# Every pair of a 512-token chunk takes seven products, and four of its accumulators are copied out before the joins

## The chip, the cores and the metric

The kernel runs on one core of one Trainium2 chip. A core has TensorE (PE: matrix products, with a weight load of its own, PEld), VectorE (DVE), ScalarE (ACT), GpSimd (POOL) and queues that issue transfers (SP's among them). Each takes its instructions in the order in which the program wrote them, and they meet at semaphores. The metric is the device time of one execution in microseconds, as the median of several runs.

## The reference

Two stages stand one behind the other. The first is a Fourier mix: `X = rfft(x)` along 3008 tokens, `Yr = Xr @ w_r - Xi @ w_i + b_r` and `Yi = Xr @ w_i + Xi @ w_r + b_i`, a soft threshold at 0.01 on both, and `irfft`. The second works on all 4 x 3008 = 12032 tokens of 256 channels: `h = x @ w_in` (256 to 2048), `g = max(h, 0) + alpha * min(h, 0)`, `out = g @ w_out` (2048 to 256). All of it is float32. The change touches the second stage alone.

## The kernel before

Every product is made of three matmuls in a faster float format: a number is split into a high and a low part, and high x high, high x low and low x high are summed in PSUM. Splitting is work for the other engines: ScalarE copies a tile into the high format, VectorE or GpSimd subtracts that copy from the tile and so gets the low part.

The first 700 us or so hold the Fourier mix of all four batches and the second stage for 12 chunks of 256 or 384 tokens. Then come 14 chunks of 512 tokens (`n` from 0 to 13) and one of 384 tokens. The change is in these.

A chunk of 512 tokens is done in 8 *pairs* of 128-wide feature blocks (`t` from 0 to 7). One turn `k` of the last loop of the program writes, in this order:

- `s_l1` of pair `k`, the first layer: 2 x 6 matmuls of 512 columns on TensorE into two PSUM banks `ps_h` (a pool of two, L785). ScalarE takes `Relu(-ps)` from each bank (L788) and VectorE makes `g` from that and the bank (L789, "the activation"). That VectorE instruction is the last reader of its bank, and the first layer of the next pair needs the bank again.
- `s_l2` of pair `k - 2`, the second layer. The two feature blocks, the two halves of the tokens and the two halves of the output channels make a 2 x 2 by 2 x 2 block product, done by Winograd's scheme in 7 products instead of 8. Each product is 3 matmuls of 256 columns (L886 to L888): 21 matmuls. They add into seven halves of four banks over the 8 pairs of a chunk: `a[0]`, `a[1]`, `b[0]`, `b[1]` (tag `o`), `c[0]`, `c[1]` (tag `f`), and `o_last[0]`.
- `s_out`, behind the last pair of a chunk: ScalarE copies three accumulators to SBUF (L911 to L913), VectorE joins all of them to the four blocks of the output (L914 to L921, eight instructions).
- `s_sums` of pair `k`: from the activation `g` the operands of the 7 products are made. ScalarE writes the high part `dh` of three of the four blocks (L804), VectorE the sums `t13` (L816) and `t24` (L818, L820) and the low part `dl` (L819); ScalarE the high parts `h13` (L821) and `h24` (L822) of the sums, VectorE `l13` (L823) and GpSimd `l24` (L824). The high and the low tiles have two buffers each, so pair `k` writes where pair `k - 2` is read by the products of the same turn.
- `s_turn`, two turns after `s_out`: four transposes of the joined blocks (L930), whose result is then stored.

In some turns the 16 matmuls of a down-transform (L611) that brings new tokens stand ahead of `s_l1`.

One pair of each chunk is *plain*: `t = 1` (`PLAIN = (1,)`). It takes 8 ordinary block products, 24 matmuls, no `t13`, `t24`, `h24`, `l24`, and half of `h13` and `l13` (L807 to L809). Its sums are made in the very turn that has the `s_out` of the chunk before. Because two of its products go to the fourth quarter block alone, it uses an eighth accumulator, `o_last[1]`.

Of the kernel before, what the change touches and what calls it, by code (L numbers as in the profile page):

```python
# [93 lines left out]
def fft_mix_moe(ctx, tc, x, w_r, w_i, b_r, b_i, w_in, w_out, alpha, la, rb, lc, rd, lf, cf, sel, out):  # L94
# [38 lines left out]
    def f(t):  # L133
        return t.bitcast(F32)
# [599 lines left out]
    HS = SC // 2  # L734
# [55 lines left out]
                                   op0=ALU.mult, op1=ALU.add)  # L790
        sq[n, t] = q

    def s_sums(n, t):
        q = sq.pop((n, t))
        if n == NS2 - 1:
            z_parts(t, q)
# [6 lines left out]
        l13 = work.tile([128, 2, HS], F32R, tag="Yh", name="l13")  # L803
        A.activation(out=dh, in_=q[:, HS:], func=AF.Copy)  # L804
        d = [(dh[:, HS * k:HS * k + HS], dl[:, HS * k:HS * k + HS]) for k in range(3)]
        if t in PLAIN:
            A.activation(out=h13[:, 0], in_=b12, func=AF.Copy)  # L807
            V.tensor_tensor(out=dl, in0=q[:, HS:], in1=f(dh), op=ALU.subtract)
            V.tensor_tensor(out=l13[:, 0], in0=b12, in1=f(h13)[:, 0], op=ALU.subtract)  # L809
            sg[n, t] = d + [(h13[:, 0], l13[:, 0])]  # L810
            return
        t13 = work.tile([128, 2, HS], F32, tag="zst", name="t13")
        t24 = work.tile([128, 2, HS], F32, tag="bt", name="t24", bufs=3)
        h24 = work.tile([128, 2, HS], F32R, tag="xl", name="h24")
# [4 lines left out]
        V.tensor_tensor(out=dl, in0=q[:, HS:], in1=f(dh), op=ALU.subtract)  # L819
        V.tensor_tensor(out=t24[:, 1], in0=b21, in1=t24[:, 0], op=ALU.subtract)  # L820
        A.activation(out=h13, in_=t13, func=AF.Copy)  # L821
        A.activation(out=h24, in_=t24, func=AF.Copy)  # L822
        V.tensor_tensor(out=l13, in0=t13, in1=f(h13), op=ALU.subtract)  # L823
        G.tensor_tensor(out=l24, in0=t24, in1=f(h24), op=ALU.subtract)  # L824
# [47 lines left out]
    def s_l2(n, t):  # L872
        if t == 0:
            sa[n] = [ps_o.tile([128, 2, HS], F32, tag="o", name="ps_o") for _ in range(2)] \
                + [ps_f.tile([128, 2, HS], F32, tag="f", name="ps_o")]
        a, b, c = sa[n]
        r, z = t == 0, t == PR - 1

        def block(j, h):
            m = 2 * t + j  # L880
            w = wo_h[m // FH][:, m % FH].rearrange("p w (c h) -> p w h c", h=2)
            return w[:, 0, h], w[:, 1, h]

        def run(prods):
            for (wh, wl), (gh, gl), o, first, last in prods:
                PE.matmul(o, wh, gh, start=first, stop=False)  # L886
                PE.matmul(o, wl, gh, start=False, stop=False)  # L887
                PE.matmul(o, wh, gl, start=False, stop=last)  # L888

        if t in PLAIN:  # L890
            b11, b22, b21, b12 = sg.pop((n, t))
            run([(block(j, h), g, o, False, False) for h, bs, o in (
                (0, (b11, b21), a[:, 1]), (0, (b12, b22), b[:, 0]),
                (1, (b11, b21), o_last[:, 0]), (1, (b12, b22), o_last[:, 1])) for j, g in enumerate(bs)])
            return
        b11, b22, b21, t1, t3, t2, t4 = sg.pop((n, t))
        s1, s2, s3, s4 = ([x[:, t] for x in sw[k]] for k in range(4))
        run([(block(0, 0), b11, a[:, 0], r, False), (block(1, 0), b21, a[:, 1], False, z),
             (s4, b22, b[:, 0], r, False), (s3, t3, b[:, 1], False, z),
             (s1, t1, c[:, 1], r, False), (s2, t2, c[:, 0], False, z),  # L900
             (block(1, 1), t4, o_last[:, 0], r, z)])

    so = {}

    def s_out(n):
        a, b, c = sa.pop(n)
        e = [work.tile([128, HS], F32, tag="q", name="se", bufs=3) for _ in range(3)]
        u = [work.tile([128, HS], F32, tag="gh", name="su", bufs=4) for _ in range(4)]
        c1 = work.tile([128, 2, HS], F32, tag="Yt", name="c1", bufs=1)
        c2 = work.tile([128, 2, HS], F32, tag="Yc", name="c2", bufs=1)  # L910
        A.activation(out=e[0], in_=a[:, 0], func=AF.Copy)  # L911
        A.activation(out=e[1], in_=c[:, 1], func=AF.Copy)
        A.activation(out=e[2], in_=o_last[:, 1], func=AF.Copy)  # L913
        V.tensor_tensor(out=c1[:, 1], in0=a[:, 1], in1=e[0], op=ALU.add)  # L914
        V.tensor_tensor(out=u[0], in0=c[:, 0], in1=e[0], op=ALU.add)
        V.tensor_tensor(out=u[1], in0=e[2], in1=e[1], op=ALU.subtract)
        V.tensor_tensor(out=u[2], in0=u[0], in1=e[1], op=ALU.subtract)
        V.tensor_tensor(out=u[3], in0=b[:, 1], in1=u[0], op=ALU.add)
        V.tensor_tensor(out=c1[:, 0], in0=b[:, 0], in1=u[2], op=ALU.add)
        V.tensor_tensor(out=c2[:, 1], in0=o_last[:, 0], in1=u[3], op=ALU.add)  # L920
        V.tensor_tensor(out=c2[:, 0], in0=u[3], in1=u[1], op=ALU.add)  # L921
        so[n] = c1, c2

    def s_turn(n):
# [31 lines left out]
    BO = {1: 49, 2: 86, 3: 123}  # L956
    BP = 3
    SLAG = 2
    PLAIN = (1,)
    MP = [3, 4, 4, 4, 4, 5, 5, 6]  # L960
    CM = 8
    BL = 4
# [19 lines left out]
    with tc.manual_schedule():  # L982
# [199 lines left out]
        for i in range(NS):  # L1182
# [7 lines left out]
            if i < NS - 1:  # L1190
                do(todo, i)
        for k in range(len(spairs) + SLAG):
            do(pre, k)
            if k < len(spairs):
                s_l1(*spairs[k])
# [6 lines left out]
            if k >= SLAG:  # L1202
                n, t = spairs[k - SLAG]
                if n == NS2 - 1:
                    z_l2(t)
                else:
                    s_l2(n, t)
                    if t == PR - 1:
                        s_out(n)
            if k < len(spairs):  # L1210
                s_sums(*spairs[k])
            if k >= SLAG and t == 1 and n:
                s_turn(n - 1)
        assert not pre and not post
# [32 lines left out]
```

## Time and profile before

| | us |
|---|---|
| median of 3 runs | 1357.33 (1357.21 to 1358.26) |
| the profiled execution, whole | 1358.56 |
| its span, first to last instruction | 1356.8 |
| PE busy, share of the span | 1341.8 (99%) |
| DVE busy | 1036.9 (76%) |
| ACT busy | 760.7 (56%) |
| POOL busy | 382.7 (28%) |

A matmul's row is longer than the time until the next one starts, since they overlap: a matmul of 256 columns has a row of 0.28 us, and the next starts about 0.12 us later. So the cost of a product on TensorE is read from the starts, not from the rows. A row of VectorE or ScalarE that stands for several instructions has "x2", "x4" behind it; "idle before" in brackets is the time that the engine stood still, and what ended it.

### The profile page before, as it was taken

The numbers are of one execution on the slowest core, as the hardware profiler recorded it, in microseconds if no ns is written. First come the engines' busy times: TensorE is split into PE (matmuls) and PEld (weight loads), VectorE is DVE, ScalarE is ACT, GpSimd is POOL, SyncE is SP. The second block draws the span as 40 slices with busy tenths as digits, with TensorE's granted clock in tenths as the row PEclk, the third lists the DMA queues.
The fourth block names the chain that finished last, engine by engine and source line by source line (L and its number), as shares of the span: only waits on it lengthen the run. The fifth ranks groups of instructions, "written<-read, shape, count | busy, mean of one in ns | idle before, by whom it ended". The sixth has DMA issues, their size and how long they took to land.

```text
span 1356.8 us, 25103 instructions
## 1 busy us (share of the span) xinstructions
PE 1341.8 (99%) x9208; PEld 1253.9 (92%) x9208; DVE 1036.9 (76%) x1930; ACT 760.7 (56%) x1528; POOL 382.7 (28%) x404
## 2 busy tenths in 40 slices
PE   9999999999999999999999999999999999999998
PEld 5979899999999999999999999999999999999998
DVE  2766856777777777776768888888888888888885
ACT  3566555565566645545556555555565555555553
POOL 4855832222222222222212211212112111211222
PEclk9999999999999999999999999999999999999999
DMA  9965223342334322111110110110011101110001
GB/s 239 255 176 154 80 83 109 91 135 90 100 97 130 94 68 82 47 59 47 36 36 1 39 28 1 40 28 19 13 37 29 28 6 35 28 28 8 21 17 28
DMA packets 88118, 89.66 MB, mean 66 GB/s; under 512 B 42317, under 2 KB 70448, under 8 KB 87995
## 3 DMA queue, kind: packets, MB, share of 16 engines
q1 hardware_dynamic: 79428, 76.76, 20.0%
q0 software_dynamic: 5168, 8.02, 2.3%
q10 hardware_dynamic: 3399, 3.27, 0.8%
q8 instruction: 73, 1.20, 0.4%
q14 instruction: 50, 0.41, 0.1%
HBM read 50.49 MB, written 34.34 MB: 63 GB/s over the span
## 4 chain that ended last, share of the span: by engine, by line
PE 92%; DVE 2%; DMA 2%; ACT 1%; issue 1%; POOL 0%; ACTq 0%; SPq 0%; DVEq 0%; POOLq 0%
PE ps_h L785 24%; PE ps_h L680 13%; PE ps_m L486 6%; PE ps_o L887 6%; PE ps_o L888 6%; PE ps_o L886 6%; PE ps_d L611 4%; PE ps_o L719 3%; PE ps_o L718 3%; PE ps_o L717 3%; PE ps_b L426 3%; PE ps_a L387 2%; PE o_last L719 1%; PE o_last L717 1%; PE o_last L718 1%; PE o_last L886 1%
## 5 line engine op out<-in xcount | busy, mean ns | idle before, releaser
L785 PE MATMUL ps_h<-yh,w 128*128 128x512 f32 (+1 forms) x960 | 315.6, 389 | 0.0
L824 POOL TENSOR_TENSOR l<-t,h 128x512 fp32r<-128x512 f32 x98 | 127.1, 1297 | 496.5 <-ACT h L822 452.7
L785 PEld LDWEIGHTS ps_h<-yh,w 128*128 128x128 f32 x960 | 180.0, 188 | 33.2
L789 DVE SCALAR_TENSOR_TENSOR sq<-sq,beta_s,ps_h 128x512 f32<-128x512 f32 (+1 forms) x240 | 168.0, 733 | 55.1 <-ACT sq L788 54.4
L680 PE MATMUL ps_h<-yh,w 128*128 128x384 f32 (+1 forms) x704 | 206.0, 335 | 1.3 <-DVE q L687 1.2
L785 PE MATMUL ps_h<-yl,w 128*128 128x512 f32 (+1 forms) x480 | 186.3, 388 | 0.0
L691 ACT ACTIVATE gh<-q 128x384 fp32r<-128x384 f32 (+1 forms) x192 | 99.2, 516 | 145.9 <-DVE q L687 144.6
L687 DVE SCALAR_TENSOR_TENSOR q<-q,beta_s,ps_h 128x384 f32<-128x384 f32 (+1 forms) x192 | 115.5, 601 | 81.8 <-ACT q L686 80.2
L692 POOL TENSOR_TENSOR gl<-q,gh 128x384 fp32r<-128x384 f32 (+1 forms) x91 | 98.3, 1081 | 266.6 <-ACT gh L691 253.4
L804 ACT ACTIVATE dh<-sq 128x768 fp32r<-128x768 f32 x112 | 94.8, 846 | 118.0 <-DVE sq L789 74.9
L788 ACT ACTIVATE sq<-ps_h 128x512 f32<-128x512 f32 (+1 forms) x240 | 133.2, 586 | 27.4 <-PE ps_h L785 25.9
L680 PEld LDWEIGHTS ps_h<-yh,w 128*128 128x128 f32 x704 | 129.3, 189 | 3.9 <-issue 1.3
L822 ACT ACTIVATE h<-t 128x512 fp32r<-128x512 f32 x98 | 62.0, 633 | 104.4 <-DVE t L820 101.1
L680 PE MATMUL ps_h<-yl,w 128*128 128x384 f32 (+1 forms) x352 | 116.4, 331 | 0.0
L686 ACT ACTIVATE q<-ps_h 128x384 f32<-128x384 f32 (+1 forms) x192 | 91.6, 477 | 39.5 <-PE ps_h L680 36.8
L719 PE MATMUL ps_o<-w,gl 128*128 128x256 f32 x384 | 108.5, 283 | 3.3 <-POOL gl L692 3.3
L718 PE MATMUL ps_o<-w,gh 128*128 128x256 f32 x384 | 108.4, 282 | 0.0
L717 PE MATMUL ps_o<-w,gh 128*128 128x256 f32 x384 | 108.1, 282 | 0.0
L785 PEld LDWEIGHTS ps_h<-yl,w 128*128 128x128 f32 x480 | 90.5, 189 | 13.6
L819 DVE TENSOR_TENSOR dl<-sq,dh 128x768 fp32r<-128x768 f32 x98 | 93.4, 953 | 3.7 <-ACT dh L804 3.6
L888 PE MATMUL ps_o<-l,sw_a 128*128 128x256 f32 x294 | 82.0, 279 | 0.0
L886 PE MATMUL ps_o<-h,sw_a 128*128 128x256 f32 x294 | 81.9, 279 | 0.0
(211 smaller groups left out, 3628.7 us busy)
## 6 DMA issues: line engine op xcount, KB each, us to landing
zt<-zd SPq DMA_DIRECT2D x32, 384.0 KB
ad<-ast SPq DMA_DIRECT2D x48, 192.0 KB
bt<-ad SPq DMA_DIRECT2D x72, 128.0 KB
zd<-zst SPq DMA_DIRECT2D x36, 256.0 KB
xt<-in_x SPq DMA_DIRECT2D x21, 320.0 KB
out<-oT SPq DMA_DIRECT2D x152, 32.0 KB
cw_s<-in_moe_w_in SPq DMA_DIRECT2D x8, 512.0 KB
cw_s<-in_moe_w_out SPq DMA_DIRECT2D x8, 512.0 KB
```

The lines of the kernel that those rows point to most:

```text
L680: PE.matmul(ps, wi_h[m // FH][:, w, ct, 128 * (m % FH):128 * (m % FH) + 128], a[:, ct, 0:n], start=(k == 0), stop=(k == 3 * CT - 1))
L687: V.scalar_tensor_tensor(out=q, in0=q, scalar=beta_s[:, m:m + 1], in1=ps, op0=ALU.mult, op1=ALU.add)
L691: A.activation(out=hi, in_=q, func=AF.Copy)
L717: PE.matmul(a, hi[:, t], w[:, 0], start=(i, k) in first, stop=False)
L718: PE.matmul(a, hi[:, t], w[:, 1], start=False, stop=False)
L719: PE.matmul(a, lo[:, t], w[:, 0], start=False, stop=(i, k) in last)
L785: PE.matmul(ps, wi_h[m // FH][:, w, ct, 128 * (m % FH):128 * (m % FH) + 128], a[:, ct, 0:w1], start=(k == 0), stop=(k == 3 * CT - 1))
L788: A.activation(out=q[:, j], in_=ps, func=AF.Relu, scale=-1.0)
L789: V.scalar_tensor_tensor(out=q[:, j], in0=q[:, j], scalar=beta_s[:, m:m + 1], in1=ps, op0=ALU.mult, op1=ALU.add)
L824: G.tensor_tensor(out=l24, in0=t24, in1=f(h24), op=ALU.subtract)
L886: PE.matmul(o, wh, gh, start=first, stop=False)
L888: PE.matmul(o, wh, gl, start=False, stop=last)
```

## The change

- `PLAIN` goes: all 8 pairs of a chunk take 7 products. `o_last[1]` is no longer used by them.
- The 7 products are written in another order: first the one to `o_last[0]`, then `c[1]`, `c[0]`, `a[0]`, `a[1]`, `b[0]`, `b[1]`. Before it was `a[0]`, `a[1]`, `b[0]`, `b[1]`, `c[1]`, `c[0]`, `o_last[0]`.
- `s_out` is cut in two. ScalarE now makes four copies (`a[0]`, `c[1]`, `o_last[0]`, `b[0]`), written inside `s_sums` between `h13` and `h24`; VectorE's joins are seven instead of eight, and stand behind all of `s_sums`. The copies go to four buffers of another tag.
- In the turns of the 384-token chunk, whose `s_sums` is another function, the copies stand ahead of it.

```diff
-        if t in PLAIN:
-            A.activation(out=h13[:, 0], in_=b12, func=AF.Copy)
-            V.tensor_tensor(out=dl, in0=q[:, HS:], in1=f(dh), op=ALU.subtract)
-            V.tensor_tensor(out=l13[:, 0], in0=b12, in1=f(h13)[:, 0], op=ALU.subtract)
-            sg[n, t] = d + [(h13[:, 0], l13[:, 0])]
-            return
...
         A.activation(out=h13, in_=t13, func=AF.Copy)
+        if ends is not None:
+            s_copy(ends)
         A.activation(out=h24, in_=t24, func=AF.Copy)
...
-        if t in PLAIN:
-            b11, b22, b21, b12 = sg.pop((n, t))
-            run([(block(j, h), g, o, False, False) for h, bs, o in (
-                (0, (b11, b21), a[:, 1]), (0, (b12, b22), b[:, 0]),
-                (1, (b11, b21), o_last[:, 0]), (1, (b12, b22), o_last[:, 1])) for j, g in enumerate(bs)])
-            return
...
-        run([(block(0, 0), b11, a[:, 0], r, False), (block(1, 0), b21, a[:, 1], False, z),
-             (s4, b22, b[:, 0], r, False), (s3, t3, b[:, 1], False, z),
+        run([(block(1, 1), t4, o_last[:, 0], r, z),
              (s1, t1, c[:, 1], r, False), (s2, t2, c[:, 0], False, z),
-             (block(1, 1), t4, o_last[:, 0], r, z)])
+             (block(0, 0), b11, a[:, 0], r, False), (block(1, 0), b21, a[:, 1], False, z),
+             (s4, b22, b[:, 0], r, False), (s3, t3, b[:, 1], False, z)])
...
+    def s_copy(n):
+
+        a, b, c = sa[n]
+        se[n] = []
+        for p in (a[:, 0], c[:, 1], o_last[:, 0], b[:, 0]):
+            t = work.tile([128, HS], F32, tag="gl", name="se", bufs=4)
+            A.activation(out=t, in_=p, func=AF.Copy)
+            se[n].append(t)
 
     def s_out(n):
...
-        A.activation(out=e[0], in_=a[:, 0], func=AF.Copy)
-        A.activation(out=e[1], in_=c[:, 1], func=AF.Copy)
-        A.activation(out=e[2], in_=o_last[:, 1], func=AF.Copy)
-        V.tensor_tensor(out=c1[:, 1], in0=a[:, 1], in1=e[0], op=ALU.add)
-        V.tensor_tensor(out=u[0], in0=c[:, 0], in1=e[0], op=ALU.add)
-        V.tensor_tensor(out=u[1], in0=e[2], in1=e[1], op=ALU.subtract)
-        V.tensor_tensor(out=u[2], in0=u[0], in1=e[1], op=ALU.subtract)
-        V.tensor_tensor(out=u[3], in0=b[:, 1], in1=u[0], op=ALU.add)
-        V.tensor_tensor(out=c1[:, 0], in0=b[:, 0], in1=u[2], op=ALU.add)
-        V.tensor_tensor(out=c2[:, 1], in0=o_last[:, 0], in1=u[3], op=ALU.add)
-        V.tensor_tensor(out=c2[:, 0], in0=u[3], in1=u[1], op=ALU.add)
+        for o, x, y, op in ((u2, c[:, 0], p1, ALU.add), (c1[:, 1], a[:, 1], p1, ALU.add),
+                            (u3, b[:, 1], u2, ALU.add), (u4, u2, p5, ALU.subtract),
+                            (c2[:, 1], u3, p4, ALU.add), (c1[:, 0], u4, p3, ALU.add),
+                            (c2[:, 0], u3, p5, ALU.subtract)):
+            V.tensor_tensor(out=o, in0=x, in1=y, op=op)
...
-    PLAIN = (1,)
...
                     s_l2(n, t)
-                    if t == PR - 1:
-                        s_out(n)
+                    ends = n if t == PR - 1 else None
             if k < len(spairs):
-                s_sums(*spairs[k])
+                last = spairs[k][0] == NS2 - 1
+                if last and ends is not None:
+                    s_copy(ends)
+                s_sums(*spairs[k], None if last else ends)
+            if ends is not None:
+                s_out(ends)
```

What the change does to the order on the engines is shown at one place, the turn in which the last products of chunk 1 and the sums of pair 1 of chunk 2 stand together; it is the same in the other chunks. On VectorE, before: the activations of the pair (L789), the eight joins (L914 to L921), the two low parts of the plain pair, and the next pair's activations.

```order
L789 SCALAR_TENSOR_TENSOR sq<-sq,beta_s,ps_h 128x512 x2
L914 TENSOR_TENSOR c_9807<-ps_o,se 128x256
L915 TENSOR_TENSOR su<-ps_o,se 128x256
L916 TENSOR_TENSOR su<-se 128x256
L917 TENSOR_TENSOR su<-su,se 128x256
L918 TENSOR_TENSOR su<-ps_o,su 128x256
L919 TENSOR_TENSOR c_9807<-ps_o,su 128x256
L920 TENSOR_TENSOR c_9808<-o_last,su 128x256
L921 TENSOR_TENSOR c_9808<-su 128x256
L808 TENSOR_TENSOR dl<-sq,dh 128x768
L809 TENSOR_TENSOR l_9823<-sq,h_9822 128x256
L789 SCALAR_TENSOR_TENSOR sq<-sq,beta_s,ps_h 128x512 x2
```

The same place on VectorE after the change, from the sum `t24` of the pair on (its `t13`, L810, and the activations stand ahead of these rows): L812 to L819 are the five instructions that every pair has now, L916 are the joins.

```order
L812 TENSOR_TENSOR t_9818<-sq,t_9817 128x256
L813 TENSOR_TENSOR dl<-sq,dh 128x768
L814 TENSOR_TENSOR t_9818<-sq,t_9818 128x256
L819 TENSOR_TENSOR l_9815<-t_9817,h_9814 128x512
L916 TENSOR_TENSOR su<-ps_o,se 128x256
L916 TENSOR_TENSOR c_9840<-ps_o,se 128x256
L916 TENSOR_TENSOR su<-ps_o,su 128x256
L916 TENSOR_TENSOR su<-su,se 128x256
L916 TENSOR_TENSOR c_9841<-su,se 128x256
L916 TENSOR_TENSOR c_9840<-su,se 128x256
L916 TENSOR_TENSOR c_9841<-su,se 128x256
L789 SCALAR_TENSOR_TENSOR sq<-sq,beta_s,ps_h 128x512 x2
```

Between the activations of one pair and those of the next there stood 8 + 2 instructions; now there are 5 + 7, and the joins have moved from the front of this stretch to its end.

On ScalarE, before: the two Relu of the pair (L788), three copies (L911 to L913), the high parts of the plain pair, and the next pair's Relu.

```order
L788 ACTIVATE sq<-ps_h 128x512 x2
L911 ACTIVATE se<-ps_o 128x256
L912 ACTIVATE se<-ps_o 128x256
L913 ACTIVATE se<-o_last 128x256
L804 ACTIVATE dh<-sq 128x768
L807 ACTIVATE h_9822<-sq 128x256
L788 ACTIVATE sq<-ps_h 128x512 x2
```

The same place after the change: `dh` (L804), `h13` (L815), four copies (L903), `h24` (L818).

```order
L788 ACTIVATE sq<-ps_h 128x512 x2
L804 ACTIVATE dh<-sq 128x768
L815 ACTIVATE h_9814<-t_9817 128x512
L903 ACTIVATE se<-ps_o 128x256 x2
L903 ACTIVATE se<-o_last 128x256
L903 ACTIVATE se<-ps_o 128x256
L818 ACTIVATE h_9819<-t_9818 128x512
L788 ACTIVATE sq<-ps_h 128x512 x2
```

The copies stand behind `dh` and `h13` now and ahead of `h24`. On TensorE the end of a pair's products, before:

```order
L888 MATMUL ps_o<-l_9746,sw_a 128x256
L886 MATMUL ps_o<-h_9750,sw_a 128x256
L887 MATMUL ps_o<-h_9750,sw_a 128x256
L888 MATMUL ps_o<-l_9751,sw_a 128x256
L886 MATMUL o_last<-h_9750,w_253 128x256
L887 MATMUL o_last<-h_9750,w_253 128x256
L888 MATMUL o_last<-l_9751,w_253 128x256
L785 MATMUL ps_h<-yh,w_253 128x512
```

and after, with `h_9757` as `h13` and `dh` as the high part of the three blocks of that pair:

```order
L884 MATMUL ps_o<-dl,w_253 128x256
L882 MATMUL ps_o<-dh,sw_a 128x256
L883 MATMUL ps_o<-dh,sw_b 128x256
L884 MATMUL ps_o<-dl,sw_a 128x256
L882 MATMUL ps_o<-h_9757,sw_a 128x256
L883 MATMUL ps_o<-h_9757,sw_b 128x256
L884 MATMUL ps_o<-l_9758,sw_a 128x256
L785 MATMUL ps_h<-yh,w_253 128x512
```

The tiles `dh` and `dl` were read by products 1 to 3 of 7; now they are read by products 4 to 6.

## Rows read from the trace of the kernel before

**Rows 1.** Busy time by stretch: length, busy of each engine (instructions), clock, DMA.

```profile
157.05:160.46 3.41, 3.23 (x12) 3.23 (x13) 1.84 (x3) 1.01 (x2) 2.99 (x4) 0.50 0.00 0
...
108.00:113.00 5.00, 3.83 (x31) 3.65 (x30) 2.71 (x8) 2.77 (x10) 1.90 (x4) 1.00 0.93 320
699.00:1320.00 621.00, 621.00 (x4017) 566.87 (x4016) 533.63 (x1005) 360.71 (x697) 127.36 (x99) 1.00 0.10 24
```

**Rows 2.** Timeline of TensorE, chunk 2: start us, length us, engine, line, operation.

```profile
782.39 0.40 PE L785 MATMUL ps_h<-yh,w 128*128 128x512 f32 x1
...
785.14 0.28 PE L886 MATMUL ps_o<-dh,w 128*128 128x256 f32 x1
...
787.62 0.40 PE L785 MATMUL ps_h<-yh,w 128*128 128x512 f32 x1
...
795.60 0.28 PE L886 MATMUL ps_o<-dh,w 128*128 128x256 f32 x1
...
798.23 0.28 PE L887 MATMUL o_last<-dh,w 128*128 128x256 f32 x1
...
798.47 0.39 PE L785 MATMUL ps_h<-yh,w 128*128 128x512 f32 x1
...
803.69 1.92 PE L611 MATMUL ps_d<-rd_s,zt 96*128 96x94 f32 x16
805.40 0.48 PE L785 MATMUL ps_h<-yh,w 128*128 128x512 f32 x1
```

**Rows 3.** Groups by line from 600 us on: xcount | busy, mean ns | idle before.

```profile
L808 DVE TENSOR_TENSOR dl<-sq,dh 128x768 fp32r<-128x768 f32 x14 | 13.3, 952 | 1.3 <-ACT dh L804 1.3
```

**Rows 4.** Timeline of VectorE over one ordinary pair.

```profile
826.47 1.40 DVE L789 SCALAR_TENSOR_TENSOR sq<-sq,beta_s,ps_h 128x512 f32<-128x512 f32 x2 [0.67 <-ACT sq L788]
...
830.25 0.68 DVE L823 TENSOR_TENSOR l<-t,h 128x512 fp32r<-128x512 f32 x1
831.60 0.75 DVE L789 SCALAR_TENSOR_TENSOR sq<-sq,beta_s,ps_h 128x512 f32<-128x512 f32 x1 [0.67 <-ACT sq L788]
```

**Rows 5.** Timeline of VectorE in chunk 2: joins, plain pair, transposes.

```profile
785.23 1.50 DVE L789 SCALAR_TENSOR_TENSOR sq<-sq,beta_s,ps_h 128x512 f32<-128x512 f32 x2 [0.67 <-ACT sq L788]
...
787.87 0.42 DVE L915 TENSOR_TENSOR su<-ps_o,se 128x256 f32<-128x256 f32 x1 [0.81 <-ACT se L912]
...
790.24 0.95 DVE L808 TENSOR_TENSOR dl<-sq,dh 128x768 fp32r<-128x768 f32 x1
...
800.64 0.68 DVE L823 TENSOR_TENSOR l<-t,h 128x512 fp32r<-128x512 f32 x1
801.24 1.42 DVE L930 STREAM_TRANSPOSE oT<-c 128x256 f32<-128x256 f32 x4
802.59 1.36 DVE L789 SCALAR_TENSOR_TENSOR sq<-sq,beta_s,ps_h 128x512 f32<-128x512 f32 x2
```

**Rows 6.** Timeline of ScalarE: a copy, a high part, a pair's Relu.

```profile
787.82 0.38 ACT L913 ACTIVATE se<-o_last 128x256 f32<-128x256 f32 x1
...
798.55 0.85 ACT L804 ACTIVATE dh<-sq 128x768 fp32r<-128x768 f32 x1 [1.54 <-PE o_last L887]
...
830.99 1.07 ACT L788 ACTIVATE sq<-ps_h 128x512 f32<-128x512 f32 x2
```

**Rows 7.** Timeline of all engines at pair 1 of chunk 5.

```profile
918.08 0.40 PE L785 MATMUL ps_h<-yh,w 128*128 128x512 f32 x1
...
921.67 0.75 DVE L789 SCALAR_TENSOR_TENSOR sq<-sq,beta_s,ps_h 128x512 f32<-128x512 f32 x1 [0.66 <-ACT sq L788]
```

**Rows 8.** Timeline of all engines where TensorE waits for a bank.

```profile
110.69 0.48 DVE L687 SCALAR_TENSOR_TENSOR q<-q,beta_s,ps_h 128x256 f32<-128x256 f32 x1
...
111.31 0.41 PE L680 MATMUL ps_h<-yh,w 128*128 128x384 f32 x1 [1.18 <-DVE q L687]
...
111.56 0.34 PE L680 MATMUL ps_h<-yl,w 128*128 128x384 f32 x1
```

**Rows 9.** Timeline of TensorE at its longest wait behind the start.

```profile
157.23 0.58 PE L719 MATMUL ps_o<-w,gl 128*128 128x256 f32 x1 [2.62 <-POOL gl L692]
```

More of the change, by code (lines that the diff above doesn't have):

```diff
@@ L791, in s_l1, with s_sums @@
         sq[n, t] = q
-    def s_sums(n, t):
+    def s_sums(n, t, ends=None):
         q = sq.pop((n, t))
@@ L900, in s_l2 @@
              (s1, t1, c[:, 1], r, False), (s2, t2, c[:, 0], False, z),
-             (block(1, 1), t4, o_last[:, 0], r, z)])
+             (block(0, 0), b11, a[:, 0], r, False), (block(1, 0), b21, a[:, 1], False, z),
+             (s4, b22, b[:, 0], r, False), (s3, t3, b[:, 1], False, z)])
     so = {}
+    se = {}
+    def s_copy(n):
[5 more added lines that the diff above has]
+            se[n].append(t)
@@ L905, in s_out @@
     def s_out(n):
         a, b, c = sa.pop(n)
-        e = [work.tile([128, HS], F32, tag="q", name="se", bufs=3) for _ in range(3)]
-        u = [work.tile([128, HS], F32, tag="gh", name="su", bufs=4) for _ in range(4)]
+        p1, p5, p4, p3 = se.pop(n)
+        u2, u3, u4 = (work.tile([128, HS], F32, tag="gh", name="su", bufs=4) for _ in range(3))
         c1 = work.tile([128, 2, HS], F32, tag="Yt", name="c1", bufs=1)
         c2 = work.tile([128, 2, HS], F32, tag="Yc", name="c2", bufs=1)
-        A.activation(out=e[0], in_=a[:, 0], func=AF.Copy)
@@ L1192, in fft_mix_moe @@
         for k in range(len(spairs) + SLAG):
+            ends = None
             do(pre, k)
```

## The prediction, made before the changed kernel was run

> **What bounds the kernel now.** I read the busy times by stretch first. From 699 to 1320 us, where all 512-token chunks lie, TensorE is busy for 621.00 of 621.00 us at the full one of its two clocks, 2.4 GHz (granted 1.00), VectorE for 534, ScalarE for 361 [rows 1]. So nothing that another engine saves can shorten this stretch; only less work on TensorE can, and only as long as nobody makes it wait. The next view is TensorE's timeline, read by starts. A pair takes 782.39 to 787.62 = 5.23 us, of which its 21 second-layer matmuls take 785.14 to 787.62 = 2.48. The plain pair's 24 take 795.60 to 798.47 = 2.87 [rows 2]. The third is VectorE over one ordinary pair: from one activation to the next it is 831.60 - 826.47 = 5.13 us [rows 4]. That is only 0.10 less than TensorE's 5.23. VectorE is therefore a second bound that lies just under the first, and the question is what it has to carry at a chunk's end.
>
> **What goes.** 14 plain pairs [rows 3] at 2.87 - 2.48 = 0.39 us: 5.5 us less on TensorE. This much is certain if TensorE never stands still.
>
> **What comes back.** The plain pair is not only dearer on TensorE, it is cheaper on VectorE, and its sums fall in the very turn that holds the joins. There VectorE loses one join and two low parts and gets the five instructions of a full pair. I work out when the first activation behind the joins is done, because the second next first layer needs the bank that it reads. On VectorE, behind the start of a pair's first activation: its l13 starts 830.25 - 826.47 = 3.78 later [rows 4], and the next instruction can start 801.24 - 800.64 = 0.60 behind that [rows 5]; the seven joins take what seven instructions take before, 787.87 to 790.24 = 2.37 [rows 5]; the activation takes 0.75 [rows 4]. The hand-over to TensorE I take from the one place where it waited for such a bank: the activation ended at 110.69 + 0.48 = 111.17, TensorE started at 111.31, so 0.14 [rows 8]. The nearest other hand-over, TensorE to ScalarE, bounds it from below: 798.23 + 0.28 = 798.51 to 798.55, 0.04 [rows 2, 6]. I take 0.14, since it is the same pair of engines and the same kind of wait.
>
> Path 1, VectorE being late. If the pair's first activation starts L behind its first layer, the bank is free at L + 3.78 + 0.60 + 2.37 + 0.75 + 0.14 = L + 7.64; TensorE wants it at 2 x 5.23 = 10.46. It stands still for L - 2.82. In chunk 2, L is 785.23 - 782.39 = 2.84 [rows 2, 5]; in chunk 5 it is 921.67 - 918.08 = 3.59 [rows 7]; in the 13 chunks that follow another one it lies between 2.83 and 3.59, and is over 3.27 in five of them.
>
> Path 2, a wait that the change adds. `dh` is written over a buffer that the products of the same turn read. Before, product 3 of 7 was its last reader, now it is product 6, whose second matmul is the 17th of the 21. ScalarE takes `dh` 0.04 after such a matmul [rows 2, 6]. Behind `dh`, ScalarE has h13, the copies, h24 and the next pair's Relu queued, VectorE has dl, l13, the joins and that activation. From the start of the products: 16 x 2.48 / 21 = 1.89, + 0.28 + 0.04 = 2.21 until `dh` starts; l13 starts 800.64 - 798.55 = 2.09 behind it in a pair where `dh` was late [rows 5, 6]; then 0.60 + 2.37 + 0.75 + 0.14: 8.16. TensorE wants the bank at 2.48 + 5.23 = 7.71. It stands still for 0.45 even where VectorE has no lag. In the other turns there are no joins (2.37 less), and this wait costs nothing.
>
> So the stall at each of the 13 joins is the larger of 0.45 and L - 2.82: eight times 0.45, five times 0.48 to 0.77, 6.9 in all (0.53 each). A matmul that has waited starts slowly: the one at 111.31 has a row of 0.41 against 0.34 for the next [rows 8]; 13 x 0.07 = 0.9. That is 7.8 us at this place. The 14th plain pair opens the first chunk, where there is nothing to join; I take 0 there.
>
> A second place follows. When TensorE restarts, VectorE is exactly late: the next activations start 0.89 before, 4.24 behind (5.13 on) and, past the pair with the four transposes (802.59 - 801.24 = 1.35 [rows 5]), at 4.24 + 3.78 + 0.60 + 1.35 = 9.97. With 0.89 the bank is free at 10.86; TensorE wants it at 10.46 + 0.07. Another 0.33, with the slow start 0.40. In six of the 13 chunks the 16 down-transform matmuls stand just there and give 805.40 - 803.69 = 1.71 [rows 2]; seven remain: 2.8 us.
>
> **What I cost at nothing.** The fourth copy and its place: four copies of 0.38 are 1.5 us, and if all of it came ahead of the next Relu (830.99 [rows 6]), the activation could start at 831.60 + 1.5 = 833.1; VectorE, busy with joins, arrives at 830.85 + 2.37 = 833.2. Covered, by 0.1 at worst. The accumulators: behind the products' start, `o_last` is free once the third copy ends, by 2.21 + 0.85 + 0.63 + 3 x 0.38 = 4.8 (the middle term, for h13, is my estimate from the Relu of that width, 1.07 for two [rows 6]); the next chunk writes it at 2.48 + 2.75 = 5.23. `a` is free with the second join, 2.21 + 2.09 + 0.60 + 0.34 + 0.42 + 0.14 = 5.8, and wanted nine matmuls on, at 6.3. `b` comes later still. Where path 1 is later than path 2, by 0.3 at most, this still holds, with 0.2 left. GpSimd's l24 is now read by the first product instead of the last two, a pair and a half after it is made; its 14 more instructions fall in its idle time (127 us busy of 621 [rows 1]).
>
> **Sum.** 7.8 + 2.8 - 5.5 = +5.1 us: 1363.7 against the profiled execution's 1358.56. The median of the runs shown lies 1.23 below that execution, so I forecast 1357.33 + 5.1 = 1362.4. Ends: with a hand-over of 0.04 and no slow start the stalls are 13 x 0.43 + 7 x 0.23 = 7.2, the sum +1.7, 1359.0. If each join took its whole row of 0.42 (7 x 0.42 = 2.94 instead of 2.37), 7.4 more come at the first place: 1369.8. I stay near the middle because the joins are written so that neighbours don't wait for each other.
>
> **Rivals.**
> *Shorter waits.* The same two places, with the price at its lower end: 1359.0, within 0.2%. For it: the balance is fine, a mean stall of 0.39 per chunk already eats the gain. Against: the only wait of this kind cost 0.14 and a slow start [rows 8].
> *No stall.* VectorE is early enough, and only the 5.5 us remain: 1351.8. The mechanism would be that the copies are now ahead of the joins, so that VectorE no longer waits for ScalarE among them (0.81 at 787.87 [rows 5]), and gains on TensorE by 0.10 in each pair. It decides at the turn of the joins: they would have to end 0.45 earlier than in path 2 and L to stay under 2.82. For it: L is close to that in several chunks. Against: path 2 doesn't hang on how early VectorE is, and the 0.81 was a wait in a turn with little else to do.
> *The clock.* The wait of 2.62 at 157.23 [rows 9] was followed by 3.41 us at the lower clock, 1.2 GHz (granted 0.50), while that of 1.18 at 111.31 [rows 8] lies in a stretch at 1.00 [rows 1]. If each of the 20 stalls cost such a stretch, half of 3.41 would be lost 20 times: +34, 1396. Against: the stalls are 0.4 to 0.8 long. The Trainium skill (TensorE: Matmul & The Clock Gate, "A second HAM failure mode: psum-queue depth-cycling") says that short idle times between groups of matmuls, as a kernel goes round its PSUM banks, can make the clock swing between both levels. By that rule this rival is the one to come; the trace shows it for the long wait alone, and no row shows it for a short one.
>
> **How the numbers follow.** The forecast 0.61, shorter waits 0.21, no stall 0.14, the clock 0.04. What a measurement of this kernel can tell from no change is 0.2%, 2.7 us. Slower is the forecast and the clock, 0.65; the same is the shorter waits, 0.21; faster is no stall, 0.14. The forecast's own range is 1359 to 1368. To leave out no more than 2 in 10 it has to reach down past the shorter waits to part of the way to no stall, 1354; above, I stop at 1368, short of the upper end of the joins.
>
> **What would show it.** TensorE's idle time by line should be new at L785 alone, with VectorE's L789 as its cause, some 0.4 to 0.8 us at pair 3 of every chunk and again at pair 5 where no down-transform stands ahead; between these, pairs of 5.23. VectorE's first activation behind the joins should start about 4.8 to 5.1 us behind its first layer. `dh` should wait for TensorE's L883 in the turn of the joins. No matmul at L882 to L884 should wait. I am wrong if those activations start under 4.3 us behind, if the first product of a chunk waits for a copy or a join, or if the clock falls.

## The result, and the profile after

The changed kernel takes 1369.26 us (median of 4 runs, 1367.84 to 1369.72) against 1357.80 for the kernel before (4 runs beside it): ratio 1.0083, 95% interval 1.0065 to 1.0100. It is slower, as forecast, but by 11.5 us where 5.1 were forecast, and it lies above the range. The profiled span is 1367.6 us, 10.8 longer. The mean granted clock is 0.998, and 1.00 in the stretch of the 512-token chunks, so the 1.2 GHz level has no part in it. The row shows the length of the stretch, busy time of TensorE, its loads, VectorE, ScalarE and GpSimd, the clock and DMA:

```profile
710.00:1330.00 620.00, 609.74 (x3913) 553.83 (x3912) 548.88 (x1020) 359.86 (x711) 142.39 (x111) 1.00 0.09 22
```

Before, TensorE was busy for all of such a stretch [rows 1]; now it stands still for 10.3 of 620 us.

The page gives the busy time by engine. VectorE is busy for 23.6 us more than before and GpSimd for 17.4; TensorE has 42 matmuls less.

```profile
PE 1340.3 (98%) x9166; PEld 1249.6 (91%) x9166; DVE 1060.5 (78%) x1958; ACT 766.9 (56%) x1556; POOL 400.1 (29%) x418
```

Then the chain that ended last, by engine. Before, TensorE held 92% of it and VectorE 2%; now VectorE is on it for 9%.

```profile
PE 84%; DVE 9%; issue 3%; ACT 2%; DMA 1%; DVEq 0%; POOL 0%; ACTq 0%; SPq 0%
```

The third view is the groups by line, for TensorE's first layer: busy time and mean ns, then the idle time before it. Before, no idle time stood here.

```profile
L785 PE MATMUL ps_h<-yh,w 128*128 128x512 f32 (+1 forms) x960 | 317.2, 391 | 11.4 <-DVE sq L789 10.9
```

That row undercounts, since a matmul's length in the trace covers part of a short gap. I therefore read the starts in TensorE's timeline, group by group, and split the difference of the two spans. Place 1 is the first layer of a chunk's pair 3 and place 2 that of pair 5, the two places of the prediction:

| Part | us |
|---|---|
| second-layer products, 112 groups: 277.9 against 242.7 + 40.2 (98 ordinary, 14 plain) | -4.95 |
| place 1: 13 waits of 0.87 to 1.09 | +11.8 |
| place 2: 7 waits of 0.20 to 0.24 | +1.6 |
| the turn of the last chunk: one wait | +1.3 |
| slow first matmuls behind these 21 waits, 0.10 each | +2.2 |
| first layers apart from that, 120 groups, 0.011 shorter each | -1.4 |
| before the first of these layers | +0.3 |
| sum | +10.8 |

So every wait of the 512-token chunks is one that the prediction named, but the first place costs 13.1 us with its slow starts, not 7.8. Chunk 2 shows why. These are the start of a pair's products (L882) and the first layers of three pairs in TensorE's timeline (start, length, engine, line):

```profile
785.47 0.28 PE L882 MATMUL o_last<-h,w 128*128 128x256 f32 x1
...
787.95 0.40 PE L785 MATMUL ps_h<-yh,w 128*128 128x512 f32 x1
...
794.03 0.50 PE L785 MATMUL ps_h<-yh,w 128*128 128x512 f32 x1 [0.71 <-DVE sq L789]
...
799.38 0.40 PE L785 MATMUL ps_h<-yh,w 128*128 128x512 f32 x1
```

From 787.95 to 794.03 are 6.08 us, and 5.35 to the next, where an undisturbed pair takes 5.21. This is VectorE in the same turn, from l13 (L819) over the seven joins (L916) to the activation (L789) for which TensorE waits:

```profile
789.82 0.68 DVE L819 TENSOR_TENSOR l<-t,h 128x512 fp32r<-128x512 f32 x1
790.42 0.42 DVE L916 TENSOR_TENSOR su<-ps_o,se 128x256 f32<-128x256 f32 x1
790.75 0.41 DVE L916 TENSOR_TENSOR c<-ps_o,se 128x256 f32<-128x256 f32 x1
791.08 0.41 DVE L916 TENSOR_TENSOR su<-ps_o,su 128x256 f32<-128x256 f32 x1
791.41 0.90 DVE L916 TENSOR_TENSOR su<-su,se 128x256 f32<-128x256 f32 x1
792.24 1.08 DVE L916 TENSOR_TENSOR c<-su,se 128x256 f32<-128x256 f32 x3
793.24 1.39 DVE L789 SCALAR_TENSOR_TENSOR sq<-sq,beta_s,ps_h 128x512 f32<-128x512 f32 x2
```

One instruction is out of line: the fourth join takes 0.90 where its neighbours take 0.41, and the seven take 793.24 - 790.42 = 2.82 us, not 2.37. GpSimd beside it is at l24 (L820), from 790.74 to 792.04:

```profile
790.74 1.30 POOL L820 TENSOR_TENSOR l<-t,h 128x512 fp32r<-128x512 f32 x1 [3.85 <-ACT h L818]
```

The view of line L916 gives all 14 turns (shortest, median, longest in ns). Only `su<-su,se` is stretched. It is the first join that reads both inputs from SBUF; the three ahead of it read one from a PSUM bank, and the three behind it come when l24 is done. Its one short case, 408, is the last turn, where no l24 runs. In the other 13 turns it starts 0.64 to 0.71 behind the start of l24, and in every one it ends 0.28 to 0.29 behind l24's end: its end goes with GpSimd's instruction and not with its own start.

```profile
L916 DVE TENSOR_TENSOR c<-su,se x42: 409/411/415, 747.7 to 1335.7; 128x256 f32<-128x256 f32 x42
L916 DVE TENSOR_TENSOR su<-ps_o,se x14: 413/418/421, 745.8 to 1333.7; 128x256 f32<-128x256 f32 x14
...
L916 DVE TENSOR_TENSOR su<-ps_o,su x14: 407/414/418, 746.5 to 1334.4; 128x256 f32<-128x256 f32 x14
L916 DVE TENSOR_TENSOR su<-su,se x14: 408/932/949, 746.8 to 1334.7; 128x256 f32<-128x256 f32 x14
```

ScalarE in that turn shows the wait that the change adds: `dh` stands until TensorE's L883, which is product 6.

```profile
787.68 0.85 ACT L804 ACTIVATE dh<-sq 128x768 fp32r<-128x768 f32 x1 [1.20 <-PE ps_o L883]
```

The wait that the prediction didn't have lies in the first pair of the last chunk (384 tokens). ScalarE makes the four copies (L903) ahead of that pair's high parts (L827):

```profile
1330.68 0.66 ACT L903 ACTIVATE se<-ps_o 128x256 f32<-128x256 f32 x2 [1.30 <-PE ps_o L884]
...
1331.75 0.96 ACT L827 ACTIVATE zg<-sq 128x384 fp32r<-128x384 f32 x2
```

VectorE needs these for the low part (L828), which stands ahead of the joins:

```profile
1332.74 1.06 DVE L828 TENSOR_TENSOR zg<-sq,zg 128x384 fp32r<-128x384 f32 x1 [2.71 <-ACT zg L827]
1333.72 0.41 DVE L916 TENSOR_TENSOR su<-ps_o,se 128x256 f32<-128x256 f32 x1
...
1334.72 0.41 DVE L916 TENSOR_TENSOR su<-su,se 128x256 f32<-128x256 f32 x1
...
1336.06 1.12 DVE L789 SCALAR_TENSOR_TENSOR sq<-sq,beta_s,ps_h 128x384 f32<-128x384 f32 x2
```

TensorE waits for that activation:

```profile
1336.71 0.44 PE L785 MATMUL ps_h<-yh,w 128*128 128x384 f32 x1 [1.14 <-DVE sq L789]
```

VectorE stands idle for 2.71 us and does the joins only behind the low part; TensorE's next first layer starts at 1336.71, 1.42 behind the start of its last product, where 0.12 is usual.

### The profile page after: what moved, and what is told of

Same layout as the page of the kernel before. It is cut to its first block, busy times and chain, and to the rows that moved or that the text cites. A ratio compares the mean times of both kernels' runs of the same rounds, so it can differ in the third digit from the quotient of the medians.

```text
span 1367.6 us, 25199 instructions
## 1 busy us (share of the span) xinstructions
PE 1340.3 (98%) x9166; PEld 1249.6 (91%) x9166; DVE 1060.5 (78%) x1958; ACT 766.9 (56%) x1556; POOL 400.1 (29%) x418
## 4 chain that ended last, share of the span: by engine, by line
PE 84%; DVE 9%; issue 3%; ACT 2%; DMA 1%; DVEq 0%; POOL 0%; ACTq 0%; SPq 0%
PE ps_h L785 20%; PE ps_h L680 13%; PE ps_m L486 6%; PE ps_o L882 4%; PE ps_o L883 4%; PE ps_o L884 4%; PE ps_d L611 4%; PE ps_o L719 3%; PE ps_o L718 3%; PE ps_b L426 3%; PE ps_o L717 3%; PE ps_m L473 3%; DVE sq L789 2%; DVE su L916 2%; PE o_last L719 1%
## 5 line engine op out<-in xcount | busy, mean ns | idle before, releaser
L785 PE MATMUL ps_h<-yh,w 128*128 128x512 f32 (+1 forms) x960 | 317.2, 391 | 11.4 <-DVE sq L789 10.9
L820 POOL TENSOR_TENSOR l<-t,h 128x512 fp32r<-128x512 f32 x112 | 145.2, 1297 | 487.8 <-ACT h L818 463.6
L785 PEld LDWEIGHTS ps_h<-yh,w 128*128 128x128 f32 x960 | 180.0, 188 | 47.6 <-DVE sq L789 15.6
L789 DVE SCALAR_TENSOR_TENSOR sq<-sq,beta_s,ps_h 128x512 f32<-128x512 f32 (+1 forms) x240 | 167.0, 732 | 50.2 <-ACT sq L788 49.6
L785 PE MATMUL ps_h<-yl,w 128*128 128x512 f32 (+1 forms) x480 | 185.8, 387 | 0.0
L804 ACT ACTIVATE dh<-sq 128x768 fp32r<-128x768 f32 x112 | 94.9, 848 | 153.7 <-DVE sq L789 98.0
L788 ACT ACTIVATE sq<-ps_h 128x512 f32<-128x512 f32 (+1 forms) x240 | 129.7, 587 | 11.4 <-PE ps_h L785 8.3
L818 ACT ACTIVATE h<-t 128x512 fp32r<-128x512 f32 x112 | 71.0, 634 | 104.4 <-DVE t L814 104.4
L813 DVE TENSOR_TENSOR dl<-sq,dh 128x768 fp32r<-128x768 f32 x112 | 106.8, 953 | 0.4
L785 PEld LDWEIGHTS ps_h<-yl,w 128*128 128x128 f32 x480 | 90.2, 188 | 13.6
L882 PE MATMUL ps_o<-h,sw_a 128*128 128x256 f32 x336 | 94.4, 281 | 0.0
L884 PE MATMUL ps_o<-l,sw_a 128*128 128x256 f32 x336 | 93.1, 277 | 0.0
```

The costliest lines, as they stand in the source:

```text
L785: PE.matmul(ps, wi_h[m // FH][:, w, ct, 128 * (m % FH):128 * (m % FH) + 128], a[:, ct, 0:w1], start=(k == 0), stop=(k == 3 * CT - 1))
L788: A.activation(out=q[:, j], in_=ps, func=AF.Relu, scale=-1.0)
L789: V.scalar_tensor_tensor(out=q[:, j], in0=q[:, j], scalar=beta_s[:, m:m + 1], in1=ps, op0=ALU.mult, op1=ALU.add)
```

## The experiments

Theory A is the same throughout: the time is lost where TensorE waits for the activation behind the joins, and the excess over the forecast is the fourth join, held up while GpSimd works on l24. Eight kernels were run in two groups, each timed beside the kernel before (1357.68 in the first group, 1358.16 in the second).

**e1: no l24 beside the joins.** In the turn of the joins l24 is left out (those products read l13's tile as their low part, so this part of the computation is changed).

```
-        l24 = work.tile([128, 2, HS], F32R, tag="Yl", name="l24")
+        l24 = l13 if ends is not None else work.tile([128, 2, HS], F32R, tag="Yl", name="l24")
...
-        G.tensor_tensor(out=l24, in0=t24, in1=f(h24), op=ALU.subtract)
+        if ends is None:
+            G.tensor_tensor(out=l24, in0=t24, in1=f(h24), op=ALU.subtract)
```

> Leaves out GpSimd's l24 in the turn of the joins alone (those two products read l13 as their low part). Theory A, GpSimd and VectorE shut each other out: the fourth join, 0.93 us in the changed kernel, takes 0.41 as the others; TensorE's stall at pair 3 falls from 0.91 to about 0.45 at 13 places, 5.9 us in all: 1363.4. Theory B, the fourth join waits for what it reads (the join before it, or ScalarE's copy): it stays at 0.9 and the time at 1369, within 0.5.

Measured: 1362.47 (9 runs), ratio 1.0030 [1.0020, 1.0040]. The fourth join is at 0.42 in all 14 turns:

```profile
L917 DVE TENSOR_TENSOR su<-su,se x14: 414/419/421, 746.2 to 1327.8; 128x256 f32<-128x256 f32 x14
```

The waits at place 1 fall from 0.87 to 0.35 in most chunks, 0.52 each: the length of the stretch. VectorE's instructions and their order are those of the changed kernel, so neither the length of VectorE's queue nor the dependence of the fourth join on the first explains the stretch.

**e2: the joins read banks.** The second inputs of three joins come from PSUM (three, not the four that the expectation says), so that only the last join reads two SBUF inputs; for this the joins of `c2` change places. l24 is back, and only two copies are left.

```
-        for p in (a[:, 0], c[:, 1], o_last[:, 0], b[:, 0]):
+        for p in (a[:, 0], o_last[:, 0]):
...
-        p1, p5, p4, p3 = se.pop(n)
+        p1, p4 = se.pop(n)
+        p5, p3 = c[:, 1], b[:, 0]
...
```

> All work stays, but four of the seven joins take their second operand from PSUM instead of a copy (two copies fewer), so that only the last join has both inputs in SBUF. Theory A: nothing is stretched while GpSimd makes l24, the joins take 2.35 again, the stall at pair 3 falls by 0.45 at 13 places: 1363.4. Theory B: the fourth join still stands behind the same sum and takes 0.9: 1369. If the later release of the banks b and c costs something, TensorE waits at L882 instead.

Measured: 1362.16 (10 runs), ratio 1.0031 [1.0022, 1.0040]. The join that follows the first now reads `ps_o` and takes 0.41 with l24 running beside it (the last row is GpSimd's, until 790.26):

```profile
789.66 0.41 DVE L917 TENSOR_TENSOR su<-su,ps_o 128x256 f32<-128x256 f32 x1
789.99 0.75 DVE L917 TENSOR_TENSOR c<-su,ps_o 128x256 f32<-128x256 f32 x2
790.65 0.42 DVE L917 TENSOR_TENSOR c<-su,se 128x256 f32<-128x256 f32 x1
790.99 1.41 DVE L789 SCALAR_TENSOR_TENSOR sq<-sq,beta_s,ps_h 128x512 f32<-128x512 f32 x2
```

```profile
788.96 1.30 POOL L820 TENSOR_TENSOR l<-t,h 128x512 fp32r<-128x512 f32 x1 [3.81 <-ACT h L818]
```

The seven take 790.99 - 788.67 = 2.32. e1 takes GpSimd's instruction away and e2 the second SBUF input; either ends the stretch, so it needs both. In e2 TensorE pays a part elsewhere, as expected: the products that write the banks held longer wait 13 times, 2.8 us in all by the starts.

The Trainium skill (SBUF — State Buffer, "Who interferes with whom") says that VectorE and GpSimd share a pair of SBUF ports, that a VectorE instruction with two SBUF inputs contends with a GpSimd instruction that reads SBUF, and that the one that starts first holds it for its whole length. The traces agree: in chunk 2 l24 ends at 792.04 and the fourth join at 792.31, the join ends 0.28 to 0.29 behind l24 in all 13 turns, and the joins with one PSUM input run through at 0.41. That section could have given this before the run.

**e3: the plain pair comes back.** One plain pair per chunk and the eighth accumulator are restored (now with its copy, in the new place); copies, order and joins stay as changed.

```
+        if t in PLAIN:
+            A.activation(out=h13[:, 0], in_=b12, func=AF.Copy)
+            if ends is not None:
+                s_copy(ends)
...
+    PLAIN = (1,)
```

> Only the plain pair comes back (with its eighth accumulator and a fifth copy); the order of products, the copies inside the sums and the joins behind them stay. Theory A, the wait is VectorE's load in the turn of the joins: 14 x 0.39 = 5.5 us more on TensorE, but no stall at pairs 3 and 5 (15.5 us less): 1359.3, the 1.4 us at the last chunk still in it. Theory C, the new order of products or the place of the joins makes TensorE wait by itself: stalls at pair 3 stay over 0.5 and the time stays over 1366.

Measured: 1364.09 (4 runs), ratio 1.0041 [1.0027, 1.0055], 4.8 above what theory A expected and below what the rival asked. The span is 5.0 above that of before. By the starts there are 13 waits of 0.21 on average at the same first layer (2.75), slow starts (1.4), one wait in the last chunk (2.04), longer products (0.5) and shorter first layers (-1.4), and none at place 2. The expectation had the last chunk alone. What it left out is the prediction's path 2. With a plain pair VectorE has time to spare, and now the wait of `dh` for product 6 stands alone, ahead of the low part that needs it:

```profile
788.19 0.96 DVE L810 TENSOR_TENSOR dl<-sq,dh 128x768 fp32r<-128x768 f32 x1 [1.27 <-ACT dh L804]
...
790.40 0.42 DVE L930 TENSOR_TENSOR su<-su,se 128x256 f32<-128x256 f32 x1
...
792.20 1.40 DVE L789 SCALAR_TENSOR_TENSOR sq<-sq,beta_s,ps_h 128x512 f32<-128x512 f32 x2
```

A plain pair has no l24, and here too the fourth join takes 0.42.

**e4: the joins spread.** Three joins, those with an input from a bank, stay in the turn; the other four go two by two into the next two turns, ahead of l13; the four transposes go two by two into the two turns behind those; the last chunk's copies stand behind the high parts.

```
+        joins = [(u2, c[:, 0], p1, ALU.add), (c1[:, 1], a[:, 1], p1, ALU.add), (u3, b[:, 1], u2, ALU.add)]
+        late[n] = [(u4, u2, p5, ALU.subtract), (c2[:, 1], u3, p4, ALU.add), (c1[:, 0], u4, p3, ALU.add),
+                   (c2[:, 0], u3, p5, ALU.subtract)]
...
+                for j in range(2):
+                    at(k + 1 + j, s_late, ends, j, when=extra)
+                    at(k + 3 + j, s_turn, ends, (1 - j,), when=extra)
...
```

> The work of the changed kernel, spread on VectorE: in the turn of the joins only the three joins that read PSUM; the other four two by two ahead of l13 in the next two turns, and the transposes two by two in the two turns after those; in the 384-token chunk the copies stand behind the high parts. Theory A: the activation behind the joins is 1.8 us earlier, the added pieces fit into VectorE's 0.64 us of idle time per pair, and no place waits: 1369.3 - 16.9 = 1352.4, faster than both. Theory D, VectorE's total load in a chunk is what binds: the stalls only move to later pairs, 1362 to 1369.

Measured: 1351.13 (1350.39 to 1351.18, 5 runs), ratio 0.9945 [0.9932, 0.9957]: faster than both kernels. VectorE does as much as in the changed kernel, and TensorE stands still at no first layer; the stretch of the 512-token chunks is full again:

```profile
710.00:1320.00 610.00, 610.00 (x3957) 558.65 (x3957) 549.46 (x1027) 364.85 (x722) 161.31 (x112) 1.00 0.09 23
```

So VectorE's load is not the bound by its sum (549 of 610 us); what counts is how much of it lies ahead of one activation. The edit moves joins, transposes and the last chunk's copies together and takes the fourth join away from l24, so it shows that all 21 waits go, not what each piece is worth. In chunk 2 that activation starts 0.99 behind the first join:

```profile
787.95 0.42 DVE L913 TENSOR_TENSOR su<-ps_o,se 128x256 f32<-128x256 f32 x1
788.28 0.42 DVE L913 TENSOR_TENSOR c<-ps_o,se 128x256 f32<-128x256 f32 x1
788.61 0.42 DVE L913 TENSOR_TENSOR su<-ps_o,su 128x256 f32<-128x256 f32 x1
788.94 1.40 DVE L789 SCALAR_TENSOR_TENSOR sq<-sq,beta_s,ps_h 128x512 f32<-128x512 f32 x2
```

**e5: the last chunk's copies behind its high parts.**

```
             if k < len(spairs):
                 last = spairs[k][0] == NS2 - 1
+                s_sums(*spairs[k], None if last else ends)
                 if last and ends is not None:
                     s_copy(ends)
-                s_sums(*spairs[k], None if last else ends)
```

> The changed kernel, with one thing undone: in the turn of the last chunk (384 tokens) the four copies stand behind the pair's high parts on ScalarE again, as before the change, and no longer ahead of them. Theory A (the copies hold up zg there, VectorE does the joins behind zg's low part, and TensorE waits 1.30 us once, with a slow start of 0.10): that one wait goes, 1369.3 - 1.4 = 1367.9, and the 20 waits in the 512-token chunks stay. Rival (in that turn the joins themselves are late, whatever the copies do): the wait stays, 1369.3.

Measured: 1367.56 (5 runs), ratio 1.0076 [1.0062, 1.0090]. The wait there shrinks from 1.30 to 0.80 by the starts, so A holds for under half of it. The high parts start earlier, but the joins still stand behind the low part, and the activation behind them:

```profile
1330.93 1.05 DVE L828 TENSOR_TENSOR zg<-sq,zg 128x384 fp32r<-128x384 f32 x1 [2.21 <-ACT zg L827]
1331.91 0.41 DVE L916 TENSOR_TENSOR su<-ps_o,se 128x256 f32<-128x256 f32 x1
...
1334.25 1.13 DVE L789 SCALAR_TENSOR_TENSOR sq<-sq,beta_s,ps_h 128x384 f32<-128x384 f32 x2
```

Before, the joins stood ahead of that low part, filled VectorE's wait, and TensorE did not wait there. So the place of the joins is what is left for the rest; no run moved it alone. A difference of 1.7 in the medians is near what a timing can tell; the trace carries this.

**e6: the old order of products in pairs 1 to 7.**

```
...
+        late_first = [(block(1, 1), t4, o_last[:, 0], r, z),
+             (s1, t1, c[:, 1], r, False), (s2, t2, c[:, 0], False, z)]
+        rest = [(block(0, 0), b11, a[:, 0], r, False), (block(1, 0), b21, a[:, 1], False, z),
+             (s4, b22, b[:, 0], r, False), (s3, t3, b[:, 1], False, z)]
+        run(late_first + rest if t == 0 else rest + late_first[1:] + late_first[:1])
```

> The changed kernel, with the old order of the seven products in pairs 1 to 7 of a chunk; only pair 0, which needs the banks as they come free, keeps the new one. So dh waits for the third product again in the turns of the joins. Theory A (both paths of the prediction bind at nearly the same time: the new order holds VectorE at 3.15 us or more behind the first layer in every turn, and where it is taken away VectorE's own lag, 2.83 to 3.6 us, takes over at once): in the few chunks with little lag some 0.3 us less, in the others 0.0 to 0.15, in all 1 to 3 us: 1366.3 to 1368.3. Theory B (the wait of dh alone decides at the joins): 13 waits shorter by 0.45, 1363.4. Theory C (only the length of VectorE's work counts, the order nothing): 1369.3.

Measured: 1368.70 (5 runs), ratio 1.0076 [1.0063, 1.0089]: above A's interval by 0.4, and not told apart from C by the time. B falls. In chunk 2 `dh` now waits for VectorE, and the activation behind the joins is no earlier against its first layer (793.35 - 788.03 = 5.32, in the changed kernel 793.24 - 787.95 = 5.29). The rows are from ScalarE, TensorE and VectorE:

```profile
787.68 0.85 ACT L804 ACTIVATE dh<-sq 128x768 fp32r<-128x768 f32 x1 [1.05 <-DVE sq L789]
```

```profile
788.03 0.40 PE L785 MATMUL ps_h<-yh,w 128*128 128x512 f32 x1
```

```profile
793.35 1.40 DVE L789 SCALAR_TENSOR_TENSOR sq<-sq,beta_s,ps_h 128x512 f32<-128x512 f32 x2
```

Over the 13 chunks that distance falls from a mean of 5.34 to 5.22, 1.5 us in all: the two paths of the prediction bind at nearly the same time, as A has it. It is lost again because the 120 first layers take 1.7 us more by the starts than in the changed kernel, for which I have no cause.

**e7: the spread joins with the old order.** The edit of e6 in the kernel of e4.

> The kernel with the joins spread over three turns (three in the turn of the sums, two each in the next two, the transposes in the two behind), and besides the old order of the seven products in pairs 1 to 7. Theory A (with the joins spread no bank is late, so the order of the products is free): 1351.1, as the spread kernel, TensorE without a wait at L785. Rival (the wait of dh for the sixth product costs TensorE something in every pair that no row shows): faster than 1351.1 by over 2 us.

Measured: 1352.17 (4 runs), ratio 0.9954 [0.9939, 0.9970]. Again no wait at the first layer, as A says: with the joins spread, the order of pairs 1 to 7 sets no wait. The span is 1.5 above that of e4, and the first layers are 1.8 longer, as in e6.

**e8: the kernel before, without plain pairs alone.** The old order, the place of the copies and that of the joins ahead of the low parts stay; the third copy and one join go with the eighth accumulator.

```
...
-        A.activation(out=e[2], in_=o_last[:, 1], func=AF.Copy)
-        V.tensor_tensor(out=u[1], in0=e[2], in1=e[1], op=ALU.subtract)
-        V.tensor_tensor(out=c2[:, 0], in0=u[3], in1=u[1], op=ALU.add)
+        V.tensor_tensor(out=c2[:, 0], in0=u[3], in1=e[1], op=ALU.subtract)
...
-    PLAIN = (1,)
+    PLAIN = ()
```

> The kernel before, with one part of the change alone: no plain pair (and with it no eighth accumulator). The copies, the order of the products and the place of the joins ahead of the turn's low parts stay as before. Theory A (the rest of the change pays for itself once the plain pair is gone): the joins end 5.1 us behind the start of the products, as before; the five VectorE instructions of a full pair follow, 2.95 us, then the activation and the hand-over, 0.9, so the bank is free at 8.9 to 9.0 where TensorE wants it at 7.7: 13 waits of 1.25 with the slow start 0.1, 17.5, and 2.3 at pair 5; less 5.5 for the plain pairs: 1357.8 + 14.3 = 1372. Theory B (the rest of the change costs about 5 us by itself, as it does beside a plain pair, and this without a plain pair too): 1369.3 - 5 = 1364.

Measured: 1378.57 (4 runs), ratio 1.0148 [1.0134, 1.0162]. B falls; A has the direction, and is 6.6 short. The waits at place 1 are 1.64 in 12 of 13 chunks, and those at place 2 about 0.25 as ever. The rest is a wait of VectorE that the expectation left out: without joins behind l13, the activation waits for its Relu, which ScalarE has queued behind h24:

```profile
793.14 0.69 DVE L823 TENSOR_TENSOR l<-t,h 128x512 fp32r<-128x512 f32 x1
794.49 1.41 DVE L789 SCALAR_TENSOR_TENSOR sq<-sq,beta_s,ps_h 128x512 f32<-128x512 f32 x2 [0.66 <-ACT sq L788]
```

So the other parts of the change do pay, about 9 us, once there is no plain pair; beside one (e3) they cost 5.0 by the spans. Each half of the change loses by itself, the plain pair's removal 20.4 us over the kernel before and the rest 6.4; together they lose 11.5, less than the removal alone.

## Why the prediction was too low

*What goes.* 5.5 was forecast and 4.95 measured: the 98 other groups are 0.005 longer each. The first layers gave back 1.4 that was not in the sum.

*Place 1, the step that failed.* It is the term "the seven joins take what seven instructions take before, 787.87 to 790.24 = 2.37" [rows 5], with its cover, that GpSimd's 14 more instructions "fall in its idle time" [rows 1]. The rest of path 2 came out nearly as worked: `dh` starts 787.68 - 785.47 = 2.21 behind the products (2.21), l13 2.14 behind it (2.09), the joins 0.60 behind that (0.60), and from the activation's start to TensorE are 794.03 - 793.24 = 0.79 (0.89). The joins take 2.82, 0.45 more than the 2.37 of the sum. With l13 0.05 later and the last step 0.10 shorter that makes 0.40 of the 0.42 that the usual wait, 0.87, has over the forecast 0.45. Without l24 (e1) the waits are mostly 0.35, and the whole kernel takes 1362.47. That it lies beside the forecast of 1362.4 is luck: the last chunk (1.4) and the first layers (-1.4), both left out of the sum, cancel, and by the spans e1 is 3.9 longer than the kernel before, for 5.1 forecast.

Rows 5 couldn't show the stretch. In the kernel before, what VectorE did beside the 98 l24 was the activation, the low parts of the down-transform (`yl<-ps_d,yh`), each with one input from a bank, or transposes with a single input; the joins stood in a turn whose sums, those of the plain pair, have no l24. "Its idle time" was a statement about GpSimd alone; it had to be asked which VectorE instruction stands beside it. The upper end (2.94 for the joins) had the right size for another reason, and would have given 1369.8; that I cut the range below it put the result outside.

*Path 1 against path 2.* The larger of both was the right form. Ten chunks with up to 3.33 of lag wait alike, 0.87, by path 2; those with 3.42, 3.49 and 3.55 wait 0.96, 1.03 and 1.09, by path 1. But path 2 also set the lag: with `dh` late in every turn it never falls below 3.15, where it was 2.83 before. Hence taking the wait away gained so little (e6).

*Place 2.* 2.8 was forecast and 1.6 + 0.7 = 2.3 measured, at seven chunks as forecast, those without a down-transform there. It doesn't hang on the size of the first wait (about 0.24 in e2, where that is 0.18, and 0.25 in e8, where it is 1.64): this fits the prediction's argument that TensorE restarts by that activation in every case, which leaves VectorE no margin for the transposes. In e3, where the first wait is 0.21, it is missing; there the plain pair's products, 0.39 longer, stand between the two places, and I take that for the reason.

*Slow start.* 0.07 was forecast from rows 8 and 0.10 measured (a row of 0.50 at 794.03 against 0.40).

*The last chunk.* It was not in the sum, which priced 13 joins in the 512-token chunks and none here, and cost 1.4. There the copies are ahead of the high parts and the joins behind the low part (e5 puts 0.5 on the first).

*Costed at nothing.* The copies, the accumulators and l24's new reader: no matmul at L882 to L884 waits in the 512-token chunks, so this was right.

*Signs.* TensorE's idle time is new at L785 alone, behind L789, and `dh` waits for L883, as foretold. The activation behind the joins starts 5.29 to 5.51 behind its first layer, over the 4.8 to 5.1 given, and the waits at pair 3 are 0.87 to 1.09 for 0.4 to 0.8. Of the three signs of being wrong none came: they looked for VectorE early, for a product that waits and for the clock, and not for VectorE later than forecast.

*Rivals.* The shorter waits did not come: all 13 at place 1 are longer than forecast. No stall is what e4 shows, at 1351.1 for the 1351.8 given, but by moving the joins, which the change didn't. The granted clock stayed at 1.00 through the waits of 0.20 to 1.09 in the 512-token chunks, so that rival fell. The swings between both levels that the Trainium skill speaks of (TensorE: Matmul & The Clock Gate, "A second HAM failure mode: psum-queue depth-cycling") do not come about here.

## What to carry to other kernels

Here VectorE's period lay 2% under TensorE's, and once a turn was late a further lengthening of it was paid in full: the 0.51 by which the fourth join was stretched came back as 0.52 of wait (e1), though VectorE was busy for only 549 of 620 us. So spread such work over turns before taking work from the bound engine. Before an instruction is called hidden in GpSimd's idle time, look which VectorE instructions will stand beside it, and whether they read two SBUF tiles. A duration taken from a row holds only with the neighbours of that row.

## What the runs showed of the hardware that I had not expected

- A VectorE tensor_tensor with two SBUF inputs took 0.93 us (median of 14, 13 of them beside GpSimd's tensor_tensor) instead of 0.42; with one input in PSUM it took 0.41 beside the same neighbour (e2).
- It goes the other way too. In e4 l24 starts 0.22 behind the start of l13, which reads two SBUF tiles, and takes 1.62 instead of 1.30. So it is in all 52 turns of e4 in which l24 starts while l13 runs (1.60 to 1.63); the other 60 take 1.30:

```profile
793.39 0.69 DVE L823 TENSOR_TENSOR l<-t,h 128x512 fp32r<-128x512 f32 x1
```

```profile
793.61 1.62 POOL L824 TENSOR_TENSOR l<-t,h 128x512 fp32r<-128x512 f32 x1 [4.00 <-ACT h L820]
```

- The 12 matmuls of a first layer took 2.73 us between starts behind the new order of products and 2.75 behind the old one (e6, e7 and before). The cause is open.
